# The first batch of an attention-and-maxout kernel: earlier transpositions and products with v, weights prepared at half the rate, four groups in place of six for the first 288 tokens

## The chip, the cores and the metric

The kernel runs on one core of a Trainium2 chip. The time is the device time of one execution in microseconds. The kernel before took 789.06 us in the median of three runs (788.3, 789.06 and 790.6). The profile was taken from one more execution.

A core has five engines with instruction queues of their own: TensorE (PE; its loads of the stationary operand are shown as PEld), VectorE (DVE), ScalarE (ACT), GpSimd (POOL) and SyncE (SP), which here issues most of the transfers (DMA). Every queue is worked in order, and engines wait for one another through semaphores. TensorE writes to PSUM, which is cut into banks.

## The reference

For 8 batches, 8 heads, 576 tokens and a head size of 64:

```python
scores = q @ k.T / 8  - slope[h] * |i - j|        # for 0 <= i - j < 128, else -1e9
attn   = softmax(scores)
x      = (attn @ v), heads side by side           # 4608 tokens x 512
h      = max(x @ w1, x @ w2, x @ w3)              # 512 -> 768
out    = h @ w_out                                # 768 -> 512
```

All of it is in float32. A query sees itself and the 127 tokens before it.

## The kernel before

**Attention.** A task is a batch and a pair of heads, of which a batch has four (`NP`). A task has five blocks of 128 query rows (`NB`, the last has 64). One block of one task is a *step*; a batch has 20. The first batch takes the blocks 0 to 2 of all four tasks first (steps 0 to 11, `FIRST = 3`) and then the blocks 3 and 4 (steps 12 to 19), so that its first 288 tokens are ready before the others. Steps go in pairs. `products` (L334) makes q times k for a pair, into the PSUM tile `scores` or, for every second pair of the first batch, into the banks ps_m0 and ps_m1. `score` masks (DVE, L360 and L363), adds the bias and takes the minimum (DVE, L377) and forms the exponential (ACT, L381) into a tile `p`, of which there are four. `sums_of` (L390, L393) and `normalise` (L400) divide by the sum on DVE; in the first batch block 0 is normalised together with block 1. `turn` transposes the pair on TensorE (L414), copies it out on ACT (L418, L424, L427) and cuts it to the window by two selects on POOL (L430, L434). `mix_first` multiplies with v in the first batch (L448), once for a task's first 384 tokens and once for its last 192, and copies the result to `xk` on ACT (L456). `mix` (L475, L484) does so in the later batches.

**The maxout, first batch.** The 512x768 weights of w1, w2 and w3 are cut into nine groups 0 to 8, w_out into groups 9 to 11. `plain_x(j)` splits the j-th 288 tokens of x into a high and a low part (ACT L501, DVE L502). `plain_unit` (L646) is a unit of six products of 128x128 by 128x288, three for each of two row halves of the weights: high by low, low by high, high by high. A group needs four units for 288 tokens. The units of the groups below `AHEAD` are done for the first 288 tokens, then for the second 288; from `AHEAD` on both halves of the tokens are done group by group. After 72 units come 16 of nine products each with w_out. Every second unit's result goes to DVE (L602, a maximum with the result so far) or ACT (L604).

**The maxout, later batches.** `unit` (L684) uses a scheme of seven products for eight with sums of weights and of inputs; its weights are stored in DRAM while the first two batches run and are streamed back.

**Preparing weights.** `preparing` is one list of steps that is taken up piece by piece. For each of the twelve groups of `A_ORDER` there are two conversion steps (`convert`: ACT L139, DVE L140, ACT L143, DVE L144 and L149, and a store, L150) and two splitting steps (`part`: ACT L153, DVE L154, and stores L177 or L190 to `keep`); then the group two places on is fetched (L133). Afterwards the sums are made. `weights(n, upto)` takes n steps, and more until `upto` are done. Groups 0 to 2, and those from `AHEAD` on, are split whole into a ring of two tiles; groups from 3 below `AHEAD` are split half by half into other tiles, which are free at that time. A splitting step of a group from `AHEAD` on is held back until an earlier group's units are through.

**The order of the work.** Everything is put on a list of events with a time in steps, which is sorted, and a planner takes the instructions in this order, places those that are ready by its own estimate of durations, and so makes the order of each engine's queue. In the first 64 score instructions DVE's order is tied by hand (`follow`), and TensorE's order is tied to the list from event time 50 on (`fix`). `turn` of a pair that begins at step c has the time c + 4.003, the product with v c + 6.001, `plain_x(0)` and the first unit 16.05, `plain_x(1)` 24.05. The units of the first 288 tokens are spread evenly between these two, those behind them up to unit 72 over the time to 46.05. From time 1.2 to 17.2 one step of weights is taken at every step of attention, later one with every odd unit. The functions that the change touches, and what calls them, follow.

## Time and profile before

| | |
|---|---|
| median of three runs | 789.06 us |
| the profiled execution | 785.73 us, of which the span from first to last instruction is 784.0 |
| PE busy | 751.6 us (96%) |
| PEld busy | 670.0 us (85%) |
| DVE busy | 569.5 us (73%) |
| ACT busy | 511.1 us (65%) |
| POOL busy | 171.2 us (22%) |
| transfers | 187.96 MB, 240 GB/s over the span |

A line such as L646 is a line of the kernel. A row of a group or of the timeline names the line, the engine, the operation, the tile that it writes and those that it reads, the shape and the number of instructions; the brackets or the last column say how long the engine was idle before and what it then waited for. The granted clock is the share of TensorE's full clock that the throttle let through.

### The profile page before, as it was taken

To read this page: it belongs to the slowest core of one execution; us is meant where nothing else is said; L and a number is where in the kernel's file an instruction comes from. 1 tells how busy PE (TensorE), PEld (TensorE's weight loads), DVE (VectorE), ACT (ScalarE), POOL (GpSimd) and SP (SyncE) were. 2 spreads that over 40 slices of the span, in tenths; PEclk is the share of its full clock that TensorE was granted. 3 is DMA by queue.
4 is the path that set the end of the run, shared out by engine and by line. 5 is a ranking of instruction groups with operands and counts; after the bars stand their busy time and mean duration, and the time that the engine had idled before them with its cause. 6 is when DMAs were issued, how large, how long until landed. Compare 5 with 4: busy or idle time off the path is not lost.

```text
span 784.0 us, 18084 instructions
## 1 busy us (share of the span) xinstructions
PE 751.6 (96%) x6344; PEld 670.0 (85%) x6344; DVE 569.5 (73%) x1951; ACT 511.1 (65%) x1668; POOL 171.2 (22%) x374
## 2 busy tenths in 40 slices
PE   5779999999999999999999999999999999999997
PEld 2357878888889998899989988999889998999987
DVE  5878989779999477774769567784677657673662
ACT  6867778668778666766677566775677656642331
POOL 1122222111123122212322122221222122201100
PEclk9969999999999999999999999999999999999999
DMA  8887775679897478745887379755887368756851
GB/s 295 292 272 251 231 257 199 200 243 334 303 323 272 140 268 291 263 166 202 284 292 269 118 241 310 251 204 175 293 297 251 135 211 290 243 176 207 290 192 61
DMA packets 54155, 187.96 MB, mean 240 GB/s; under 512 B 5936, under 2 KB 15664, under 8 KB 47152
## 3 DMA queue, kind: packets, MB, share of 16 engines
q0 software_dynamic: 15552, 99.10, 38.4%
q1 hardware_dynamic: 38368, 87.64, 32.5%
q8 instruction: 50, 0.82, 0.4%
q14 instruction: 41, 0.34, 0.1%
q10 hardware_dynamic: 144, 0.07, 0.0%
HBM read 154.53 MB, written 32.24 MB: 238 GB/s over the span
## 4 chain that ended last, share of the span: by engine, by line
PE 60%; DVE 16%; issue 10%; DMA 5%; ACT 5%; POOL 2%; SPq 1%; POOLq 0%; ACTq 0%; DVEq 0%
PE ps_m L684 41%; PE ps_x L475 6%; PE ps_s L334 5%; PE ps_m L646 4%; PE pt L414 4%; DMA hs<-in_w_all 3%; DVE hs L502 2%; DVE t L607 2%; DVE xs L502 2%; ACT p L381 1%; DVE s L377 1%; DVE hq L608 1%; DVE ps_s L363 1%; ACT xs L501 1%; DMA wt<-keep 1%
## 5 line engine op out<-in xcount | busy, mean ns | idle before, releaser
L684 PE MATMUL ps_m<-xs,wt 128*128 128x288 f32 x2646 | 370.4, 297 | 3.9 <-DVE t L607 1.8
L684 PEld LDWEIGHTS ps_m<-xs,wt 128*128 128x128 f32 x2646 | 355.3, 188 | 7.7 <-DVE t L607 3.4
L430 POOL TENSOR_SCALAR_AFFINE_SELECT pp<-pr 128x256 f32<-128x256 f32 (+1 forms) x128 | 56.6, 442 | 385.2 <-ACT pr L427 226.4
L381 ACT ACTIVATE p<-s,st 128x128 f32<-128x128 f32 (+1 forms) x320 | 127.0, 399 | 20.0 <-DVE st L377 18.8
L693 ACT COPY t<-ps_m 128x288 f32<-128x288 f32 x231 | 89.7, 394 | 71.8 <-PE ps_m L684 71.2
L684 PE MATMUL ps_m<-hs,ow 128*128 128x288 f32 x882 | 124.0, 297 | 1.6 <-DVE hs L502 0.8
L684 PEld LDWEIGHTS ps_m<-hs,ow 128*128 128x128 f32 x882 | 118.7, 188 | 3.1 <-ACT t L693 1.1
L285 POOL DMA_DIRECT2D wt<-keep x108 | 58.0, 537 | 193.8 <-PE ps_m L684 189.0
L405 ACT ACTIVATE p<-p,st 128x128 f32<-128x128 f32 (+1 forms) x240 | 84.0, 397 | 17.9 <-DVE st L393 17.8
L377 DVE CUSTOM_DVE_ANT_0 s<-ps_s,bias 128x128 f32<-128x128 f32 (+1 forms) x300 | 76.3, 279 | 19.4 <-PE ps_s L334 17.2
L607 DVE TENSOR_TENSOR t<-ps_m,t 128x288 f32<-128x288 f32 x126 | 56.5, 452 | 36.8 <-PE ps_m L684 20.9
L363 DVE COPY_PREDICATED ps_s<-prev,ps_s 128x256 f32<-128x256 uint8 x120 | 50.6, 421 | 40.6 <-PE ps_s L334 39.2
L334 PE MATMUL ps_s<-qk 64*64 64x192 f32 (+1 forms) x1052 | 64.8, 329 | 6.3 <-DMA qk<-in_qk 4.2
L501 ACT CAST hs<-hq 128x288 fp32r<-128x288 f32 x117 | 48.8, 429 | 29.4 <-DVE hq L608 16.7
L475 PE MATMUL ps_x<-pp,v 128*64 128x256 f32 (+3 forms) x672 | 65.3, 321 | 0.0
L434 POOL TENSOR_SCALAR_AFFINE_SELECT pp<-pr 128x256 f32<-128x256 f32 (+1 forms) x128 | 63.1, 493 | 0.0
L427 ACT COPY pr<-pt 128x256 f32<-128x256 f32 x68 | 20.2, 322 | 64.6 <-PE pt L414 64.6
L381 ACT ACTIVATION_READ_ACCUMULATOR p<-s,st 128x1 f32 (+1 forms) x320 | 61.1, 191 | 0.0
L414 PEld LDWEIGHTS pt<-ident,p 128*128 128x128 f32 (+1 forms) x320 | 34.7, 145 | 28.2 <-issue 17.4
L414 PE MATMUL pt<-ident,p 128*128 128x128 f32 (+1 forms) x320 | 57.4, 292 | 1.3 <-ACT pr L427 0.9
L608 DVE TENSOR_TENSOR hq<-t,hq 128x288 f32<-128x288 f32 x126 | 57.0, 459 | 2.0
L502 DVE TENSOR_TENSOR hs<-hq,hs 128x288 fp32r<-128x288 f32 x117 | 53.1, 460 | 6.2 <-ACT hs L501 6.2
(78 smaller groups left out, 857.7 us busy)
## 6 DMA issues: line engine op xcount, KB each, us to landing
wt<-keep POOLq DMA_DIRECT2D x54, 1024.0 KB, 7.2
wt<-keep POOLq DMA_DIRECT2D x54, 768.0 KB, 5.4
qk<-in_qk SPq DMA_DIRECT2D x29, 576.0 KB, 6.3
hs<-in_w_all SPq DMA_DIRECT2D x24, 512.0 KB, 5.2
v<-in_v SPq DMA_DIRECT2D x30, 320.0 KB, 5.5
outT<-t SPq DMA_DIRECT2D x64, 144.0 KB, 1.8
keep<-wt SPq DMA_DIRECT2D x27, 256.0 KB, 3.8
wt<-keep SPq DMA_DIRECT2D x27, 256.0 KB, 4.4
```

The source lines that it names most:

```text
L334: pe(nc.tensor.matmul(ps[j][d:d + D, o:o + k1 - k0], lhsT=qkt[t][j * D:(j + 1) * D, 0, q0:q0 + D], rhs=qkt[t][j * D:(j + 1) * D, 1, k0:k1] ...
L377: follow(nc.vector.tensor_tensor_reduce(out=s[:n], in0=ps[j][:n, P:2 * P], in1=(bias if i else bias0)[:n, 2 * hp + j, :], scale=-0.125, sc ...
L381: nc.scalar.activation(p[:n, j], s[:n], AF.Exp, bias=st[:n, 0, a, j:j + 1], scale=-1.0, accum_out=st[:n, 1, a, j:j + 1])
L405: nc.scalar.activation(p[:n, j], p[:n, j], AF.Copy, scale=st[:n, 2, a, j:j + 1])
L414: pe(nc.tensor.transpose(out=pt[:, a, j, :n], in_=p[:n, j], identity=ident[:n, :n]))
L434: nc.gpsimd.affine_select(out=w[:n, :, 0, :n], in_=r[:n, a, :, :n], pattern=[[0, 2], [1, n]], compare_op=ALU.is_ge, fill=0.0, base=0, chan ...
L475: pe(nc.tensor.matmul(x[j * D:(j + 1) * D, c:c + e - a], lhsT=vv[:n, i, j * D:(j + 1) * D], rhs=w[:n, j].rearrange("p a b -> p (a b)")[:, ...
L502: e.tensor_tensor(out=lo, in0=src, in1=hi.bitcast(F32), op=ALU.subtract)
L607: nc.vector.tensor_tensor(out=s, in0=ps, in1=e, op=ALU.add)
L608: nc.vector.tensor_tensor(out=h, in0=s, in1=h, op=ALU.max)
L684: pe(nc.tensor.matmul(ps, lhsT=lt, rhs=rt, start=i == 0 and k in (0, 1, 4), stop=i == len(pairs) - 1, skip_group_check=True,))
L693: nc.scalar.copy(out=e, in_=ps)
```

## The change

Three constants of the order are changed, all for the first batch.

- `turn` of the first batch comes at 0.1 behind the last normalisation of its two blocks (`ended`), and no longer 4.003 behind the pair's first step.
- The product with v comes 4.001 and no longer 6.001 behind it (`LAG_X0`); `plain_x(0)`, the first unit (14.05) and `plain_x(1)` (22.05) move by two steps with it. The time at which the second batch's tokens are taken up stays 46.05.
- Weights are prepared at the event times 1.2, 3.2, ... 15.2: eight steps and not seventeen.
- `AHEAD` is 4 and not 6: sixteen units and not twenty-four for the first 288 tokens, then sixteen for the second, then five groups (and not three) for both. Groups 4 and 5 are therefore split whole, into the ring.

```diff
-LAG_T, LAG_X = 4, 6
+LAG_T, LAG_X, LAG_X0 = 4, 6, 4
...
-    AHEAD = 6
+    AHEAD = 4
...
+    def ended(s):
+
+        return max(place_of[t, 1 if i == 0 else i] for t, i in steps[s:s + 2]) + 1.3
+
...
-                at(c + LAG_T + 0.003, turn, place_of[t, i])
+                at(c + LAG_T + 0.003 if b else ended(place_of[t, i]) + 0.1, turn, place_of[t, i])
...
-                    at(c + LAG_X + 0.001, mix_first, t, i == NB - 1)
+                    at(c + LAG_X0 + 0.001, mix_first, t, i == NB - 1)
...
     ready = [n_steps * (b + 1) - 2 + LAG_X + 0.05 + shift[b] for b in range(B)]
-    when = FIRST * NP - 2 + LAG_X + 0.05
+    ready[0] += LAG_X0 - LAG_X
+    when = FIRST * NP - 2 + LAG_X0 + 0.05
     at(when, plain_x, 0)
...
-    for s in range(1, FIRST * NP + LAG_X):
+    for s in range(1, FIRST * NP + LAG_X0, 2):
         at(s + 0.2, weights, 1)
```

## The prediction

> **What bounds the kernel now.** I read the page's busy shares and slices first, then the stretches of the start, then the order of TensorE's work in them, and last the groups of each engine there.

> ```profile
> PE 751.6 (96%) x6344; PEld 670.0 (85%) x6344; DVE 569.5 (73%) x1951; ACT 511.1 (65%) x1668; POOL 171.2 (22%) x374
> PE   5779999999999999999999999999999999999997
> DVE  5878989779999477774769567784677657673662
> ...
> 0.00:53.30 53.30, 34.77 (x222) 17.80 (x223) 39.48 (x162) 38.12 (x121) 12.77 (x30) 0.89 0.84 285
> 10.00:53.30 43.30, 30.58 (x174) 15.35 (x175) 35.71 (x141) 32.72 (x101) 10.47 (x20) 0.87 0.85 294
> 53.30:84.20 30.90, 28.54 (x236) 24.57 (x234) 27.76 (x89) 22.94 (x70) 5.19 (x12) 0.97 0.80 264
> 84.00:110.00 26.00, 25.30 (x227) 22.46 (x228) 24.96 (x96) 20.04 (x65) 6.72 (x12) 1.00 0.73 234
> 84.20:150.00 65.80, 63.46 (x582) 54.80 (x583) 58.81 (x216) 48.47 (x156) 15.51 (x32) 1.00 0.64 208
> 150.00:250.00 100.00, 98.93 (x858) 89.88 (x857) 91.55 (x315) 80.42 (x265) 21.25 (x38) 1.00 0.88 303
> ```

> In a row of stretches stand its length and then the busy time of PE, PEld, DVE, ACT and POOL. TensorE is idle for 32.4 of the 784.0 us, and 18.5 + 2.4 us of that lie before 84.2. Behind 84.2 it is the bound: 2.3 us idle up to 150, 1.1 in the next 100. Ahead of 84.2 the busiest engine is VectorE: 82% of 10 to 53.3, 90% of 53.3 to 84.2, 96% of 84 to 110. So the first batch waits for VectorE (DVE), and everything later for TensorE.

> What TensorE does at the two seams, and DVE's last score of steps 15 and 19:

> ```profile
> 53.34 5.90 PE L646 MATMUL ps_m<-xs,wt 128*128 128x288 f32 x36
> 76.31 0.64 PE L414 MATMUL pt<-ident,p 128*128 128x128 f32 x4
> 81.84 0.97 PE L448 MATMUL ps_x<-pp,hs 128*64 128x128 f32 x10
> 84.25 4.25 PE L646 MATMUL ps_m<-xs,wt 128*128 128x288 f32 x30 [0.73 <-DVE xs L502]
> ...
> 17.43 0.28 DVE L377 CUSTOM_DVE_ANT_0 s<-ps_s,bias 128x128 f32<-128x128 f32 x1
> 49.91 0.28 DVE L377 CUSTOM_DVE_ANT_0 s<-ps_m,bias 64x128 f32<-64x128 f32 x1
> 67.39 0.28 DVE L377 CUSTOM_DVE_ANT_0 s<-ps_m,bias 64x128 f32<-64x128 f32 x1
> ```

> No unit of the maxout starts before 53.3. The 24 units of the first 288 tokens are then through by 81.8, and at 84.25 the second 288 tokens start, having waited for their split on DVE. The last scores of the batch (step 19) were done at 67.7, yet their transposition came at 76.3 and their product with v at 81.8: 14 us of delay behind units. Steps 4 to 15 took from 17.4 to 50.2, so 11 steps at 3.0 us.

> **The change part by part.** I count by DVE's work up to the moment t* at which the second 288 tokens are ready (84.2 now).

> ```profile
> L149 DVE TENSOR_TENSOR hs<-hs 128x512 f32<-128x512 f32 x8 | 5.6, 700 | 1.2 <-ACT hs L143 1.1
> L154 DVE TENSOR_TENSOR wt<-hs,wt 128x512 fp32r<-128x512 f32 x6 | 4.1, 680 | 0.0
> L154 DVE TENSOR_TENSOR ow<-hs,ow 128x256 fp32r<-128x256 f32 x2 | 0.7, 408 | 0.0
> ...
> L149 DVE TENSOR_TENSOR hs<-hs 128x512 f32<-128x512 f32 x7 | 4.9, 699 | 1.9 <-ACT hs L143 1.9
> L140 DVE SCALAR_TENSOR_TENSOR hs<-hs 128x512 int32<-128x512 int32 x7 | 4.7, 677 | 0.0
> L154 DVE TENSOR_TENSOR ow<-hs,ow 128x256 fp32r<-128x256 f32 x10 | 4.4, 463 | 0.4 <-ACT ow L153 0.4
> L602 DVE TENSOR_TENSOR hq<-ps_m,hq 128x288 f32<-128x288 f32 x8 | 3.5, 450 | 0.8 <-PE ps_m L646 0.8
> L144 DVE TENSOR_SCALAR hs<-hs 128x512 int32<-128x512 int32 x7 | 2.9, 413 | 0.0
> L502 DVE TENSOR_TENSOR hs<-hq,hs 128x288 fp32r<-128x288 f32 x3 | 1.3, 442 | 0.0
> L154 DVE TENSOR_TENSOR xs<-hs,xs 128x256 fp32r<-128x256 f32 x2 | 0.8, 413 | 0.0
> L154 DVE TENSOR_TENSOR hs<-hs,hs 128x256 fp32r<-128x256 f32 x2 | 0.7, 406 | 0.0
> ```

> The first three rows are of 0 to 53.3, the others of 53.3 to 84.2. A conversion step costs DVE 0.68 + 0.41 + 0.70 = 1.79 us (L140, L144, L149), a splitting step 0.68, or 0.83 where it is done as two halves of 256. Before 84.2 there were 15 conversions (8 + 7) and 14 splittings (6 whole, and 16 halves): 29 steps.

> *Weights every second step, four groups.* Followed through the code: eight steps are given out ahead of the units in place of 17, and one with every odd unit; at unit 12 two more are forced, since group 3 must be there. At unit 16 that makes 18 steps: 10 conversions and 8 splittings. Until unit 24 nothing more comes, as group 4 takes the ring slot for which unit 23 must be through. So by t* DVE has 5 conversions (9.0 us) and 6 splittings (5.0 us) fewer to do. Eight units fewer mean four results fewer at 0.45 (L602) and two cuts fewer at 0.44: 2.7 us. Together **16.7 us**, and t* would be 84.2 − 16.7 = 67.5, if DVE's idle time (17.0 us before 84.2, 6.2 of it in the first 10) stays. ScalarE loses its share of the same steps and was less busy than DVE in every stretch. Each deferred step takes its two or three transfers on SP's queue along, so the loads of q, k and v that queue behind them go out no later than now.

> *Transpositions and products sooner.* No instruction is added. The transpositions of a pair are issued 0.1 behind its last normalisation and no longer up to 1.6 steps later, the product with v two steps earlier. On TensorE's queue, which is in order, they wait for L400 and the select on POOL with less other work ahead. The benefit is the 14 us tail; a transposition sooner also frees one of the four buffers `p` sooner, for which the score four steps later waits. I price this at nothing beside the 16.7, since DVE, which hides it, is the bound. Without that cover it is worth up to two steps, 6.0 us; the other bound is −3.0 us, one step, where scores of the next pair stand behind a blocked transposition. The earliest units meet one new wait: `products(14)` holds banks ps_m0 and ps_m1 until score 15, so the first unit, though issued at 14.05, can't precede nominal step 15. That keeps half of its gain of two steps, and 3.0 us are not in my sum.

> *What TensorE owes.* Eight units are done after t* and not before.

> ```profile
> 131.60 4.00 PE ps_m L646 x30
> 137.36 3.20 PE ps_m L646 x24
> ...
> L646 PE MATMUL ps_m<-hs,ow x144: 288/294/403, 148.1 to 169.8; 128*128 128x288 f32 x144
> ```

> By the two stretches of the chain a product takes 133 ns, a unit of six 0.80, so 6.4 us are owed. The last row, the products with w_out, has unit 72 at its head: it starts at 148.1. TensorE alone would gain 16.7 − 6.4 = **10.3 us**, and t* = 77.8 is where it gains nothing.

> *What DVE owes.* The 16.7 us come back before unit 72, which starts the w_out products: DVE had 58.8 us of work from 84.2 to 150, now 75.5 from 67.5. At 96%, the share that it reached from 84 to 110, this takes 78.6 us and ends at 146.1: 3.9 us gained. At 100% it is 7.0 gained, at the 89% of the whole stretch 84.5 us and 2.0 lost. I take 96%, the row of the stretch most like it, so **3.9**. Groups 4 and 5 are split whole and not in halves: 4 × 0.15, 0.6 us less on DVE, within this.

> Here is the clock, which the sum leaves alone:

> ```profile
> 40.00:45.00 5.00, 3.75 (x20) 1.81 (x18) 3.89 (x17) 2.72 (x9) 1.93 (x4) 0.50 0.98 352
> ```

> The granted clock was 0.50 while TensorE was 75% busy with attention, and the first 36 products took 164 ns each in place of 133: 1.1 us. [...]

> **The sum.** The profiled execution took 785.73 us, of which 784.0 are span. 784.0 − 3.9 = 780.1, so 781.8 with the 1.7 around it. The three runs' median is 789.06, 3.3 above the profiled one; on that scale the forecast is 789.06 − 3.9 = 785.2, say **785.0**.

> **The rivals.**
> *Full gain.* DVE needn't have all done by unit 72: if what is late is covered by units in hand, only TensorE's account counts, 10.3 us: 778.8. For it: from 150 to 250 TensorE lost 1.1 us with DVE at 92%. Against it: the steps are tied to units, and 48 of them must precede unit 72.

> *Nothing.* If the attention steps run at the latency of their loop (score, exponential, normalisation, transposition, banks) and not at DVE's rate, the freed DVE idles: half of the 16.7 remains, t* = 75.9, TensorE gains 1.9 at most and the owed work of DVE takes it: 788.5. For it:

> ```profile
> DVE st L390 <- ACT p L381: 4.6, 4, 2.0
> ACT xk L456 <- PE ps_x L448: 5.2, 5, 2.0
> ```

> These are waits from 10 to 53.3, DVE for ScalarE's exponential and ScalarE for the product. Against it: 3.0 us a step with DVE at 82% busy.

> *Slower: weights just in time.* Before, 40 steps are out at unit 48 where 32 are needed, and 48 at unit 64 where 44 are. Changed, by the same count: 30 against 32 at unit 48, 36 against 36 at unit 56, 40 against 44 at unit 64; the shortage is issued right ahead of the unit that needs it.

> ```profile
> L139 ACT ACTIVATE hs<-hs 128x512 int32<-128x512 uint32 x7 | 4.8, 681 | 0.6 <-DMA hs<-in_w_all 0.6
> L143 ACT ACTIVATE hs<-hs 128x512 int32<-128x512 f32 x7 | 4.8, 685 | 0.1
> L153 ACT CAST wt<-hs 128x512 fp32r<-128x512 f32 x6 | 3.7, 615 | 0.0
> ACT hs L139 <- DMA hs<-in_w_all: 4.9, 4, 2.6
> ```

> Two splittings cost 0.62 + 0.68 + 0.68 = 2.0 us; at unit 64 a whole group comes, 0.68 + 0.68 + 0.69 + 0.41 + 0.70 for the first conversion, 1.79 for the second and 2.0 to split: 6.9. Units 12, 48 and 64 make 10.9 us, and behind TensorE's stopped unit stand the transpositions and scores of batch 1, so DVE starves too. Uncovered, 10.9 − 3.9 = 7.0 lost, 796; half covered, 1.6 lost, 790.6; I set this case at 793. It decides once the stops at these units pass 3.9 us. For it: ScalarE already waited 4.9 us for raw weights from 84.2 to 150 (last row), with the larger lead. Against it: ScalarE and DVE may run ahead of TensorE, whose units take 0.8 us each.

> **How the numbers follow.** Forecast 0.44, full gain 0.18, nothing 0.20, slower 0.18. A difference under 0.3% (2.4 us) can't be told from none. The forecast's spread (shares of 100% to 95%, 782 to 786) and the full gain lie over that: 0.62 faster; the third case is the 0.20 of no change; the slower case gives 0.18. From 778 (full gain) to 792 (the slower case nearly half covered) the range leaves out its uncovered part and a gain beyond 11.

> **What would show it.** Right: first L646 near 44 (53.3 less 4 conversions and 3 splittings, 9.4 us) and at the latest 50; the 97th product of L646 near 67 and with it L502 of the second tokens; DVE over 95% busy from there to 146. Last score to last product with v under 8 us shows the sooner issue. Wrong: DVE idle over 8 us between 10 and the first unit (nothing gained); PE idle before L646 behind L154 at units 12, 48 or 64 (slower); L646's last unit of the first batch (its last product now starts at 169.8) less than 2 us earlier would refute the sum whatever the cause.

## The result and the profile after

The changed kernel takes 796.69 us (median of four executions, 793.49 to 799.23) against 788.68 for the kernel before (788.0 to 790.6). The ratio is 1.0091, with a 95% interval of 1.0063 to 1.0119: **slower by 0.9%**, about 8 us. I had forecast 785.0, faster, and the time lies above the top of my range (792). The profiled execution of the changed kernel is the longest of its four: 799.23 us, span 797.5. Ratios, here and below, are of executions in the fast state; two in the slow one (801.4 us of e2, 900.9 us of e11) count in the medians only.

Engine shares and slices of the changed kernel's page:

```profile
PE 761.9 (96%) x6344; PEld 675.8 (85%) x6344; DVE 568.7 (71%) x1947; ACT 510.7 (64%) x1664; POOL 176.3 (22%) x374
...
PE   5897999899999999999999999999999999999887
...
DVE  5876899689999566784778567784778567674562
```

The work is the same to a few instructions, and TensorE is busy 10 us longer. TensorE's slices differ from those before up to 80 us and in the eighth (140 to 160 us). Here are the two stretches of the first batch, first of the kernel before, then of the changed kernel (columns: length; busy time of PE, PEld, DVE, ACT, POOL; granted clock; share of the transfer engines; GB/s):

```profile
30.00:80.00 50.00, 40.60 (x295) 29.46 (x288) 42.52 (x155) 37.27 (x118) 11.49 (x24) 0.86 0.79 264
80.00:150.00 70.00, 66.98 (x625) 57.53 (x624) 63.01 (x229) 52.09 (x165) 15.51 (x32) 1.00 0.64 210
```

```profile
30.00:80.00 50.00, 43.48 (x287) 31.23 (x287) 36.70 (x141) 32.48 (x103) 14.74 (x24) 0.83 0.55 185
80.00:150.00 70.00, 63.86 (x549) 53.23 (x548) 60.35 (x210) 49.00 (x148) 16.62 (x28) 0.96 0.74 252
```

VectorE, which I took for the bound from 10 to 110 us, is *less* busy than before (36.7 of 50 us, was 42.5), and TensorE does its work at a lower clock in both stretches. So neither engine is full. The order of TensorE in the changed kernel, with the last row from its list of groups:

```profile
36.86 0.91 PE L646 MATMUL ps_m<-xs,wt 128*128 128x288 f32 x5
51.15 0.75 PE L448 MATMUL ps_x<-pp,v 128*64 128x192 f32 x6 [1.17 <-POOL pp L430]
71.75 0.44 PE L448 MATMUL ps_x<-pp,hs 128*64 128x128 f32 x4 [2.17 <-POOL pp L430]
72.87 1.32 PE L448 MATMUL ps_x<-pp,hs 128*64 128x192 f32 x8 [0.68 <-POOL pp L430]
74.11 1.81 PE L646 MATMUL ps_m<-xs,wt 128*128 128x288 f32 x6
76.10 4.82 PE L646 MATMUL ps_m<-xs,wt 128*128 128x288 f32 x24 [0.18 <-DVE xs L502]
...
L646 PE MATMUL ps_m<-hs,ow x144: 288/294/403, 156.7 to 178.4; 128*128 128x288 f32 x144
```

The first unit starts at 36.86 (was 53.34), earlier than the 44 that I named. But the second 288 tokens are there only at 76.1 (the unit at 74.1 is the first on them), not at 67.5. At 76.10, 102 of the products of L646 are done, at 84.25 before it was 144; the 42 missing ones are 42 × 0.133 = 5.6 us, so of 8.15 us at the seam 2.5 are a gain. From there to the start of the last product with w_out the changed kernel needs 178.4 − 76.1 = 102.3 us, where the kernel before with those 5.6 us added would need 85.55 + 5.6 = 91.15: 11.2 us lost. Together the first batch ends 8.6 us later, close to the difference of the medians (8.0). The profiled spans differ by 13.5; the other 4.9 lie in later batches. That remainder of the span is 614.2 us before and 619.1 after, and 614 to 619 in all the profiles below; I don't explain it.

The forecast counted VectorE's work up to the start of the second 288 tokens and let its idle time there stay at 17.0 us. From the start to the first unit on these tokens, before and changed (VectorE's busy time is the third pair):

```profile
0.00:84.25 84.25, 63.31 (x456) 42.38 (x456) 67.30 (x251) 61.11 (x190) 17.96 (x42) 0.92 0.82 278
0.00:74.11 74.11, 57.26 (x392) 35.75 (x392) 52.28 (x211) 47.68 (x154) 20.87 (x42) 0.92 0.70 240
```

Its work shrank by 15.0 us, near the 16.7 that I counted. Its idle time did not stay: it rose from 17.0 to 21.8 us.

### The profile page after: what moved, and what is told of

Its sections match the earlier page's. It is cut to its first block, busy times and chain, and to the rows that moved or that the text cites. A ratio compares the mean times of both kernels' runs of the same rounds, so it can differ in the third digit from the quotient of the medians.

```text
span 797.5 us, 18069 instructions
## 1 busy us (share of the span) xinstructions
PE 761.9 (96%) x6344; PEld 675.8 (85%) x6344; DVE 568.7 (71%) x1947; ACT 510.7 (64%) x1664; POOL 176.3 (22%) x374
## 4 chain that ended last, share of the span: by engine, by line
PE 59%; DVE 14%; issue 9%; ACT 4%; POOL 2%; DMA 2%; SPq 0%; POOLq 0%; DVEq 0%; ACTq 0%
PE ps_m L684 43%; PE ps_x L475 5%; PE ps_s L334 4%; PE pt L414 3%; PE ps_m L646 3%; DVE hs L502 2%; DVE t L607 2%; DVE xs L502 2%; ACT p L381 1%; DVE hq L608 1%; POOL pp L434 1%; DVE s L377 1%; DMA wt<-keep 1%; DVE ps_s L363 1%; ACT xs L501 1%
## 5 line engine op out<-in xcount | busy, mean ns | idle before, releaser
L684 PE MATMUL ps_m<-xs,wt 128*128 128x288 f32 x2646 | 372.0, 298 | 7.1 <-DMA wt<-keep 3.4
L684 PEld LDWEIGHTS ps_m<-xs,wt 128*128 128x128 f32 x2646 | 356.7, 189 | 11.2 <-DVE t L607 3.0
L430 POOL TENSOR_SCALAR_AFFINE_SELECT pp<-pr 128x256 f32<-128x256 f32 (+1 forms) x128 | 59.9, 468 | 388.8 <-ACT pr L427 228.5
L381 ACT ACTIVATE p<-s,st 128x128 f32<-128x128 f32 (+1 forms) x320 | 127.1, 400 | 19.8 <-DVE st L377 18.7
L377 DVE CUSTOM_DVE_ANT_0 s<-ps_s,bias 128x128 f32<-128x128 f32 (+1 forms) x300 | 76.1, 279 | 19.1 <-PE ps_s L334 17.5
L475 PE MATMUL ps_x<-pp,v 128*64 128x256 f32 (+3 forms) x672 | 67.1, 322 | 5.1 <-POOL pp L430 5.0
L334 PE MATMUL ps_s<-qk 64*64 64x192 f32 (+1 forms) x1052 | 66.8, 333 | 4.7 <-DMA qk<-in_qk 4.2
L434 POOL TENSOR_SCALAR_AFFINE_SELECT pp<-pr 128x256 f32<-128x256 f32 (+1 forms) x128 | 65.0, 508 | 0.0
L646 PE MATMUL ps_m<-xs,wt 128*128 128x288 f32 x384 | 63.5, 322 | 0.7 <-DVE wt L154 0.5
L646 PEld LDWEIGHTS ps_m<-xs,wt 128*128 128x128 f32 x384 | 57.8, 208 | 4.1 <-issue 2.5
L381 ACT ACTIVATION_READ_ACCUMULATOR p<-s,st 128x1 f32 (+1 forms) x320 | 61.2, 191 | 0.0
L475 PEld LDWEIGHTS ps_x<-pp,v 128*64 128x64 f32 (+1 forms) x672 | 38.7, 135 | 25.6 <-issue 9.0
```

Source lines behind the costliest of these rows:

```text
L334: pe(nc.tensor.matmul(ps[j][d:d + D, o:o + k1 - k0], lhsT=qkt[t][j * D:(j + 1) * D, 0, q0:q0 + D], rhs=qkt[t][j * D:(j + 1) * D, 1, k0:k1] ...
L377: follow(nc.vector.tensor_tensor_reduce(out=s[:n], in0=ps[j][:n, P:2 * P], in1=(bias if i else bias0)[:n, 2 * hp + j, :], scale=-0.125, sc ...
L381: nc.scalar.activation(p[:n, j], s[:n], AF.Exp, bias=st[:n, 0, a, j:j + 1], scale=-1.0, accum_out=st[:n, 1, a, j:j + 1])
L430: nc.gpsimd.affine_select(out=pp[t, i - 1][:, :, 1, :n], in_=r[:, a, :, :n], pattern=[[0, 2], [-1, n]], compare_op=ALU.is_gt, fill=0.0, ba ...
L434: nc.gpsimd.affine_select(out=w[:n, :, 0, :n], in_=r[:n, a, :, :n], pattern=[[0, 2], [1, n]], compare_op=ALU.is_ge, fill=0.0, base=0, chan ...
L475: pe(nc.tensor.matmul(x[j * D:(j + 1) * D, c:c + e - a], lhsT=vv[:n, i, j * D:(j + 1) * D], rhs=w[:n, j].rearrange("p a b -> p (a b)")[:, ...
```

## The experiments

Four questions were put: which of the three parts costs the time; whether it is the weights that come just in time (my slower rival) or the sooner order; what stops the engines; and what a select on POOL costs beside VectorE. The results for the first question stand in one table. "Lost clock" is (1 − mean granted clock) × span, in the median over the executions of a kernel: the time by which TensorE ran short of its full clock.

| groups first / preparation / lags | run | median us, of before | ratio [95%] | seam | last w_out | lost clock |
|---|---|---|---|---|---|---|
| 6, every step, old | before | 789.2 | 1 | 84.25 | 169.8 | 9.4 |
| 6, every step, sooner | e4 | 787.17, 789.32 | 0.9989 [0.9962, 1.0017] | 81.22 | 168.9 | 7.1 |
| 6, every second, old | e7 | 788.54, 789.22 | 0.9995 [0.9971, 1.0018] | 78.81 | 169.2 | 6.3 |
| 6, every second, sooner | e1 | 786.98, 789.32 | 0.9970 [0.9945, 0.9996] | 78.56 | 166.9 | 4.7 |
| 4, every step, old | e3 | 793.47, 789.32 | 1.0048 [1.0021, 1.0076] | 77.39 | 173.9 | 11.1 |
| 4, every step, sooner | e5 | 793.43, 789.27 | 1.0052 [1.0029, 1.0075] | 75.36 | 170.3 | 9.5 |
| 4, every second, old | e6 | **783.44**, 789.27 | **0.9928 [0.9902, 0.9954]** | 66.34 | 163.7 | 1.6 |
| 4, every second, sooner | changed | 796.69, 788.68 | 1.0091 [1.0063, 1.0119] | 74.11 | 178.4 | 14.7 |

"Seam" is the start of the first unit on the second 288 tokens, "last w_out" that of the last product with w_out in the first batch, both in the one profiled execution. The list of preparation times ends with `LAG_X0`. So "every step" is seventeen steps ahead of the units with the old lags and fifteen with the sooner ones, and "every second" is nine and eight.

### One part undone or done alone

**e1**, six groups, the rest of the change kept:

```diff
-    AHEAD = 4
+    AHEAD = 6
```

> The changed kernel with AHEAD back at 6: transpositions and products sooner, weights every second step, six groups. Theory A (the loss is the burst: with four groups four weight steps are forced at unit 64, their run on VectorE holds up POOL's select, TensorE stands 3.7 us at the product with v and then runs at half clock): by the count of steps nothing is forced behind unit 20, so no select of POOL over 2 us between 100 and 160 us, and the time is 788 or less. Rival B (the sooner issue or the thinner preparation does it, whatever the groups): 795 to 798, as changed.

Measured: 0.9970, three tenths of a per cent faster. With six groups the other two parts are harmless.

**e2**, one step of weights with each of the units 24 to 39 and not with every second, so that none has to be forced at units 48 and 64:

```diff
-        weights(v % 2, 4 * (A_ORDER.index(g) + 1) if g < 9 else 48)
+        weights(1 if 24 <= v < 40 else v % 2, 4 * (A_ORDER.index(g) + 1) if g < 9 else 48)
```

> The changed kernel, with one weight step at every unit from 24 to 39 and not at every second: eight steps earlier, so that by the count nothing is forced at units 48 and 64; everything else as changed. Theory A: the long select near 139 us and the 3.7 us stop go, the w_out products start 5 to 9 us earlier than 156.7, the time is 787 to 791. Rival B: no effect, 795 to 798. Rival C (VectorE has simply too much to do between 76 and 150 us): the same work earlier only moves the stops, 794 to 797.

Measured: 792.4 us, 1.0025 [0.9992, 1.0058]. That is 4.3 us less than the changed kernel, but not the time before: forced weights are a part of the loss at most.

**e3**, four groups alone, on the kernel before:

```diff
-    AHEAD = 6
+    AHEAD = 4
```

> The kernel before with only AHEAD = 4. By the count of steps two are forced at unit 48 and four at unit 64, just as in the changed kernel. Theory A: a run of VectorE with a select over 2 us ahead of the w_out products and a stop of TensorE of some 3 us with the half clock behind it; without the sooner start 792 to 798. Rival B: within 1 us of before, 789.

Measured: 1.0048, slower. Its seam is 6.9 us earlier than before, about the 6.4 us that the eight units moved take, so nothing is gained there, as I read it because the weights are still prepared ahead of it.

**e4**, the sooner order alone (the changed kernel with six groups and a step of weights at every step of attention):

```diff
-    AHEAD = 4
+    AHEAD = 6
...
-    for s in range(1, FIRST * NP + LAG_X0, 2):
+    for s in range(1, FIRST * NP + LAG_X0):
```

> The kernel before with only the sooner transpositions and products (six groups, a weight step at every step of attention). Theory A: no forced steps, so nothing lost, and the earlier start of the units gives 1 to 3 us: 785.5 to 788.5. Rival B, if the sooner issue does the harm: 793 to 797.

Measured: 0.9989, no difference that can be told.

**e5**, the changed kernel without the half rate (only the second edit of e4):

> The changed kernel with a weight step at every step of attention again (four groups and sooner issue kept). By the count two steps are forced at unit 48 and four at unit 64, none at unit 12. Theory A (four groups cause the loss by the forced steps at the end): 1.003 to 1.008 of before, as with four groups alone. Rival (the halved rate is what makes four groups worse): within 0.3% of before.

Measured: 1.0052, the same as e3. At full rate the sooner order makes no difference with four groups either.

**e6**, the changed kernel with the old lags:

```diff
-LAG_T, LAG_X, LAG_X0 = 4, 6, 4
+LAG_T, LAG_X, LAG_X0 = 4, 6, 6
...
-                at(c + LAG_T + 0.003 if b else ended(place_of[t, i]) + 0.1, turn, place_of[t, i])
+                at(c + LAG_T + 0.003, turn, place_of[t, i])
```

> The changed kernel with the old lags of transposition, product and first unit (four groups and the halved rate kept). By the count the same steps are forced as in the changed kernel, at units 12, 48 and 64. Theory A: 1.005 to 1.012 of before. If the sooner issue is what makes four groups worse, 1.003 or less.

Measured: 783.44 us, 0.9928 [0.9902, 0.9954], **the fastest kernel here, ahead of both**. Beside the changed kernel it differs in when transpositions, products with v and the first units are issued, and in one step of weights more ahead of the units (nine and not eight). Together that is worth 1.0091 − 0.9928 = 1.6%, 13 us.

**e7**, the half rate alone (e6 with `AHEAD = 6`):

> The kernel before with only the halved preparation (nine steps ahead of the units in place of 17; six groups, old lags). If the sooner issue is what does harm wherever preparation is halved, this is faster than with the sooner issue added (0.997): 0.988 to 0.994. If it harms only together with four groups: 0.996 to 1.000.

Measured: 0.9995, nothing. Its seam is 5.4 us earlier than before, but the last product with w_out only 0.6: what is deferred is given back. So no part alone gains, and none alone loses more than 0.5%. Four groups and the half rate gain 0.7% together; the sooner order gains a little or nothing in three of the four places of the table and costs 1.6% in the fourth.

What e6 does up to its seam, in the two stretches, in TensorE's order, and the start of its w_out products:

```profile
0.00:66.34 66.34, 50.28 (x408) 32.11 (x408) 52.68 (x215) 49.82 (x165) 19.53 (x42) 1.00 0.76 258
30.00:80.00 50.00, 43.70 (x389) 34.81 (x389) 45.40 (x175) 38.52 (x125) 14.73 (x28) 1.00 0.65 212
80.00:150.00 70.00, 65.20 (x562) 55.10 (x561) 62.90 (x214) 53.39 (x157) 16.47 (x29) 1.00 0.80 273
...
42.41 3.44 PE L646 MATMUL ps_m<-xs,wt 128*128 128x288 f32 x24
...
L646 PE MATMUL ps_m<-hs,ow x144: 288/294/402, 140.9 to 163.7; 128*128 128x288 f32 x144
```

VectorE does 45.4 us in 50 (the changed kernel 36.7), TensorE finishes 389 matmuls in the same busy time in which the changed kernel finishes 287, and the clock is full in both stretches.

### Which half of the sooner order

**e8**, only the transposition sooner (the first edit of e6 alone):

> Four groups and the halved rate, with the transpositions sooner but the old lags of the product with v and of the first unit. Theory B1 (the earlier units hold the banks ps_m0 and ps_m1 that the scores of step 18 need): 0.990 to 0.995, as with the old lags, and the second 288 tokens are split by 66 to 68 us. Theory B2 (waits without slack in the in-order queues of TensorE and ScalarE, behind transposition and product): partly worse, 0.996 to 1.004.

Measured: 784.59 us, 0.9946 [0.9927, 0.9964], with 2.3 us of lost clock: as e6.

**e9**, transposition and product with v sooner, the first units and the split of the tokens at their old times:

```diff
-    ready[0] += LAG_X0 - LAG_X
-    when = FIRST * NP - 2 + LAG_X0 + 0.05
+    when = FIRST * NP - 2 + LAG_X + 0.05
```

> The changed kernel, but the splits of x and the first units keep their old times (16.05 and 24.05); transpositions and products with v stay sooner. Theory B1: the harm is gone, 0.990 to 0.996, the products of q and k of step 18 (L334 into ps_m) are not scattered over 5 us and more between units. Theory B2: the harm stays, 1.003 to 1.010, with ScalarE's copy L456 waiting over 6 us for the product with v up to 76 us, as in the changed kernel (7.7; 2.1 with the old lags).

Measured: 790.25 us, 1.0004 [0.9988, 1.0021], lost clock 4.7. That lies between the ranges of the two theories, so neither accounts for all of the loss.

**e10**, product with v and units one step sooner and not two, transposition at its old time:

```diff
-LAG_T, LAG_X, LAG_X0 = 4, 6, 4
+LAG_T, LAG_X, LAG_X0 = 4, 6, 5
...
-                at(c + LAG_T + 0.003 if b else ended(place_of[t, i]) + 0.1, turn, place_of[t, i])
+                at(c + LAG_T + 0.003, turn, place_of[t, i])
```

> Four groups and the halved rate, old transpositions, product with v and units one step sooner and not two. Both theories: between the old lags (0.9928) and the changed kernel (1.009); if the loss comes from units ahead of step 18's scores, near the old lags, 0.990 to 0.996, since the first unit then stands behind score 15 anyway; if from the product's wait, near 1.001.

Measured: 789.07 us, 1.0008 [0.9981, 1.0036], lost clock 5.5. So the transposition is free, the product with v two steps sooner costs some 6 us (784.59 to 790.25), and the units with it another 6 (to 796.69).

One thing goes along with the first 6 us: e6 and e8 take nine steps of weights ahead of the units, e9, e10 and the changed kernel eight. No run holds this number while it moves the product. The stops shown next make it unlikely as the cause: they lie at 48 to 56 us, ahead of unit 12 (62.27), the first that one step less can hold up by my count. Between e9 and the changed kernel the number is the same.

The waits of 30 to 80 us, of the changed kernel, of e9, of e6 and of the kernel before (engine, tile, line, whom it waited for: us in total, times, longest):

```profile
ACT xk L456 <- PE ps_x L448: 7.7, 4, 3.6
PE ps_x L448 <- POOL pp L430: 5.8, 6, 2.2
DVE st L390 <- ACT p L381: 4.7, 4, 2.2
```

```profile
ACT xk L456 <- PE ps_x L448: 7.2, 6, 3.6
PE ps_x L448 <- POOL pp L430: 4.8, 7, 1.8
DVE st L390 <- ACT p L381: 4.1, 5, 1.5
```

```profile
PE ps_x L448 <- POOL pp L430: 2.9, 3, 1.7
ACT xk L456 <- PE ps_x L448: 2.1, 2, 1.2
DVE st L390 <- ACT p L381: 1.5, 2, 1.1
```

```profile
PE ps_x L448 <- POOL pp L430: 6.1, 7, 1.6
ACT xk L456 <- PE ps_x L448: 4.1, 4, 2.0
DVE st L390 <- ACT p L381: 3.6, 3, 2.0
```

Among the kernels with four groups and the half rate, the waits at L448 go with the time: 2.9 us in e6 and 1.8 in e8 (783 and 785 us), 4.2 in e10 and 4.8 in e9 (789 and 790), 5.8 in the changed kernel. The kernel before has as much of them, 6.1 us, with the old lags: they are not new, but the two parts that help take half of them away (e6), and the sooner product brings them back.

Three queues stop one another. One such place of the changed kernel, engine by engine:

```profile
48.38 1.10 POOL L430 TENSOR_SCALAR_AFFINE_SELECT pp<-pr 128x256 f32<-128x256 f32 x1 [4.50 <-ACT pr L427]
...
52.00 0.32 ACT L456 COPY xk<-ps_x 128x192 f32<-128x192 f32 x1 [3.52 <-PE ps_x L448]
...
53.13 0.16 DVE L390 TENSOR_SCALAR st<-st 64x2 f32<-64x2 f32 x1 [2.19 <-ACT p L381]
...
56.16 0.49 DVE L360 COPY_PREDICATED ps_m<-prev,ps_m 128x128 f32<-128x128 uint8 x2 [2.19 <-PE ps_m L334]
```

The selects run from 48.38 to 51.33. The product with v at the head of TensorE's queue waits for them (the 1.17 us at 51.15 above); behind it stand the products q times k of step 18, so its score comes at 56.16 (in e6 at 49.16; in e2, where the clock stayed full, at 54.34). ScalarE's copy of the product has been at the head of *its* queue since 48.5, and behind it stand the exponentials for which VectorE waits. VectorE then stands 2 × 2.19 = 4.4 us within 6; of the second 2.19, e2 has only 0.33, so most of it is the clock (below). In e6 VectorE has no gap over 0.1 us from 45.6 to 54.5. I call such a chain of stops a convoy.

The longest of the waits at L448, 2.17 us at 71.75, just ahead of the seam, has another cause beside the order. The select that it waits for lasted 2.57 us, from 69.12 on, while VectorE converted weights without a gap up to 71.42. In e2, which does the same instructions up to there, that select took 0.72 us and the wait was 0.31: the order makes such a stop possible, and timing decides whether it comes.

### The clock

The column of lost clock points at a second price. In the ten executions of e1, nine of e2 and ten of e10 the time rises by 0.97, 0.87 and 1.10 us with each us of lost clock (correlations 0.85, 0.83, 0.90); in the others by 0.3 to 1.6 (e4), and in the kernel before by 0.1 to 0.5 with correlations under 0.4. The instructions of e2 and of the changed kernel are the same in the same order on every engine until unit 24, behind the seam, and the two profiled executions agree within 0.06 us from 36 to 51.9 (earlier within 0.52). Then the clock is halved in one and not in the other; the changed kernel first, then e2:

```profile
48.50:51.91 3.41, 2.12 (x21) 0.90 (x19) 2.44 (x10) 0.00 (x0) 2.83 (x4) 1.00 0.93 272
51.91:55.32 3.41, 3.41 (x18) 2.22 (x13) 0.84 (x3) 3.32 (x9) 0.00 (x0) 0.50 0.97 383
...
54.37 1.75 PE L334 MATMUL ps_m<-xs 64*64 64x256 f32 x6
...
58.03 1.09 PE L334 MATMUL ps_s<-qk 64*64 64x128 f32 x14
```

```profile
47.33:50.74 3.41, 2.57 (x17) 1.48 (x15) 3.41 (x13) 1.20 (x6) 2.31 (x3) 1.00 0.94 281
50.74:54.15 3.41, 2.96 (x25) 1.80 (x25) 1.07 (x4) 2.11 (x7) 0.64 (x2) 1.00 0.99 386
...
53.33 0.97 PE L334 MATMUL ps_m<-xs 64*64 64x256 f32 x6
...
55.35 0.77 PE L334 MATMUL ps_s<-qk 64*64 64x128 f32 x14
```

The same instructions start 2.7 us later by 58.0. No edit lies between the two here: behind the same convoy the clock is 0.50 in one execution and 1.00 in the other. (Why the rows have these borders is told in the last section.)

So of the 13 us between e6 and the changed kernel, two prices add up: the convoys (e9 against e6: 6.8 us, with 3.1 us of lost clock), and what the sooner units add (the changed kernel against e9: 6.4 us, with 10.0 us more lost clock). That the clock costs time is shown for the 2.7 us above; for the rest of the second price it goes with the time and was not changed by itself. A rival stands beside it: in the changed kernel the products q times k of step 18 lie scattered between units, from 48.77 to 56.1 us, in e9 together, from 51.53 to 53.7, as theory B1 of the earlier units had it. No run parts the two.

### Weights just in time

The longest stop of TensorE in the changed kernel's first batch comes behind 66 units, next to unit 64, where four steps of weights are forced, as the slower rival counted:

```profile
139.10 4.15 POOL L434 TENSOR_SCALAR_AFFINE_SELECT pp<-pr 128x256 f32<-128x256 f32 x1
139.17 0.67 DVE L149 TENSOR_TENSOR hs<-hs 128x512 f32<-128x512 f32 x1
...
142.25 0.74 DVE L502 TENSOR_TENSOR xs<-xk,xs 128x576 fp32r<-128x576 f32 x1
...
143.67 0.76 PE L475 MATMUL ps_x<-pp,v 128*64 128x256 f32 x2 [3.70 <-POOL pp L430]
146.81 2.77 PE L646 MATMUL ps_m<-xs,wt 128*128 128x288 f32 x10
...
145.00:150.00 5.00, 5.00 (x28) 3.50 (x28) 1.58 (x4) 0.43 (x1) 0.00 (x0) 0.50 0.01 3
```

TensorE stands for 3.70 us, but not for the weights. It waits for a select on POOL that lasts 4.15 us (the median select takes 0.40), as long as seven VectorE instructions, six of weight steps and a split (L502), run without a gap, from 139.17 to 142.99. Behind the stop the clock is 0.50 from 144.07 to 150.90 us, which is 3.4 us of lost clock, and ten products take 277 ns each and not 133.

**e11** tells whether the forced steps alone do harm: e2's line on e6.

> Four groups, halved rate, old lags, and one weight step at every unit from 24 to 39, so that by the count nothing is forced at units 48 and 64. If the forced run of VectorE at unit 64 costs what its long selects suggest (2.1 and 3.6 us long, TensorE waiting 1.7 us): 0.989 to 0.992 of before. If the run is covered by other work of TensorE: 0.992 to 0.996.

Measured: 784.03 us, 0.9941 [0.9919, 0.9964], against e6's 0.9928: nothing gained by taking the forced steps away. In e6 the same thing happens (POOL and PE of e6):

```profile
128.21 3.56 POOL L434 TENSOR_SCALAR_AFFINE_SELECT pp<-pr 128x256 f32<-128x256 f32 x1
...
128.31 0.65 PE L475 MATMUL ps_x<-pp,v 128*64 128x256 f32 x2 [0.57 <-POOL pp L430]
132.18 0.65 PE L475 MATMUL ps_x<-pp,v 128*64 128x256 f32 x4 [1.11 <-POOL pp L430]
```

A select of 3.56 us, but TensorE has other work ahead of that product, waits 1.7 us in two pieces, and keeps its clock (1.00 from 80 to 150 us). Whether the 4.3 us that e2 gains come from this stop stays open: its profile shows 2.10 us of wait there in place of 3.70, but it was already 3.8 us ahead at the seam, before its edit.

### A select beside VectorE

Four kernels put extra work on VectorE beside the selects of batches 3 and 4, on the kernel before, behind the copy of the transposed block. **p1** adds 14 maxima of 128 elements with two operands in SBUF, **p2** the same with one of them in PSUM:

```diff
+            if 3 * NP <= steps[s][0] < 5 * NP:
+                for _ in range(14):
+                    nc.vector.tensor_tensor(out=dist, in0=r[:, 0, 0], in1=r[:, 0, 1], op=ALU.max)
```

(in p2 `in0=pt[:, 0, 0]`)

> The kernel before, with 14 more additions of work on VectorE behind each copy of a whole transposed pair in batches 3 and 4: maxima of two 128x128 operands, both in SBUF, into a tile that is no longer used. The output is the reference's. If a run of VectorE instructions with two SBUF operands holds up GpSimd's select, some selects L430 or L434 in these batches (about 340 to 520 us) last 2 to 4 us, where the kernel before has a median of 0.40.

> The same 14 maxima in the same places, but one operand is the transposed pair in PSUM. If it is the second SBUF operand that holds up the select, the selects in these batches stay near 0.40 us though VectorE is as busy; if any busy VectorE does it, they last 2 to 4 us as with two SBUF operands.

Measured, one execution each: 789.46 and 789.22 us beside 789.27; the selects of 128x256 of the second line take, from 300 to 420 us, 509 and 502 ns in the mean where the kernel before shows 484. The two hardly differ, and no select there is over 1.2 us: with instructions this small the question stays open. **p3** adds eight of the weights' own kind (L140's, 512 elements, two operands in SBUF), **p4** twelve with one operand and constants (L144's kind):

```diff
+            if 3 * NP <= steps[s][0] < 5 * NP:
+                b32 = bias.rearrange("p h k -> p (h k)").bitcast(I32)
+                for _ in range(8):
+                    nc.vector.scalar_tensor_tensor(
+                        out=b32, in0=b32, scalar=0, in1=b32, op0=ALU.logical_shift_left, op1=ALU.bitwise_or,
+                    )
```

(in p4 `range(12)` and `tensor_scalar(out=b32, in0=b32, scalar1=-1, scalar2=0, op0=ALU.bitwise_and, op1=ALU.bitwise_xor)`)

> The kernel before, with eight more operations of VectorE at each transposition of a whole pair in batches 3 and 4: the instruction of line 140 (two operands in SBUF, 512 elements), written so that it leaves its tile as it was. The output is the reference's. If long instructions with two SBUF operands, one behind the other, hold up the select: some selects of 2 us or more between 300 and 420 us. If only the other kind does: none over 1.2 us (the longest there before is 0.97).

> The same with twelve operations of the kind of line 144 (one operand in SBUF and immediates, 512 elements in 0.42 us). If this kind holds up the select: some selects of 2 us or more between 300 and 420 us. Otherwise none over 1.2 us.

Measured: 795.70 and 795.52 us, one execution each, beside 789.15. The selects from 300 to 420 us (count, then total us and mean ns) of the kernel before, of p3 (L440 is L434 there), with one place of its timeline, and of p4:

```profile
L434 POOL TENSOR_SCALAR_AFFINE_SELECT pp<-pr 128x256 f32<-128x256 f32 x15 | 7.3, 484 | 0.0
```

```profile
L440 POOL TENSOR_SCALAR_AFFINE_SELECT pp<-pr 128x256 f32<-128x256 f32 x16 | 13.1, 817 | 0.0
...
347.28 2.25 POOL L440 TENSOR_SCALAR_AFFINE_SELECT pp<-pr 128x256 f32<-128x256 f32 x1
347.31 0.68 DVE L422 SCALAR_TENSOR_TENSOR bias<-bias 128x512 int32<-128x512 int32 x1
348.58 1.49 DVE L422 SCALAR_TENSOR_TENSOR bias<-bias 128x512 int32<-128x512 int32 x2
```

```profile
L440 POOL TENSOR_SCALAR_AFFINE_SELECT pp<-pr 128x256 f32<-128x256 f32 x16 | 8.2, 515 | 0.0
```

On this line the long two-operand instructions add 0.33 us to the mean select and hold one for 2.25 us; about as much one-operand work (12 × 0.41 = 4.9 us beside 8 × 0.68 = 5.4) adds 0.03. On the first line (L430, 424 ns before) p3 has 486 and p4 528. Over both lines the mean rises from 457 ns to 653 in p3 and 519 in p4, and only p3 has a select over 1.2 us in this stretch. So VectorE's load alone does little, and long instructions of L140's kind do more. That it is their second SBUF operand is not shown: the two kinds are also different operations, each was run once, and the kernel before has one select of 2.32 us too (at 244 us). The two times are equal within what a single execution tells, so no price of a late select follows from them.

## Why the prediction was wrong

**The bound.** That VectorE's work sets the seam held where the queues let VectorE run: in e6 it is busy 91% of 30 to 80 us. It did not hold for the changed kernel, where it is busy 73%: up to the seam it stood idle 21.8 us, where the prediction's condition was that its idle time stays at 17.0. "DVE, which hides it, is the bound" was an argument from the kernel before, in which the sooner product doesn't exist yet.

**Weights every second step, four groups.** This step was right in direction and near in size, shown by e6, which does only this (with nine steps ahead and not eight): t* was put at 67.5 and is 66.34. That it lies so near is partly luck: VectorE's work fell by 14.6 us (67.30 to 52.68) and not by 16.7, and its idle time by 3.3 (17.0 to 13.7), which I had held fixed. 6.4 us owed at the seam leave 17.9 − 6.4 = 11.5 us (forecast 10.3); of these 5.4 are given back up to w_out (97.4 us in place of 85.55 + 6.4), where I had 6.4. Net 6.1 us in the profile and 5.8 between medians, for 3.9 forecast. The whole profiled spans differ by 2.3 us only (784.0 and 781.7), as the profiled execution of the kernel before is 3.5 us faster than its median of 789.27. Part of the gain goes with the clock: the kernel before loses 0.14 × 50 = 7.0 us in 30 to 80, e6 none, and my sum "leaves alone" the clock.

**Transpositions and products sooner** is the step that failed: "I price this at nothing beside the 16.7", with bounds of −3.0 and +6.0 us. It costs 13 us beside the other two parts (one step of weights goes along with it). The text named the wait (the product, in TensorE's in-order queue, behind the select on POOL) and then took "less other work ahead" for a benefit. It is the cause of the loss: with less work ahead, the product reaches the head before its input is there, and the queue behind it stops. I had not named the other in-order queue, ScalarE's, whose copy of the product stands ahead of exponentials. The lower bound, one step, was for a single blockade; the profile has six waits at L448 (5.8 us), four at L456 (7.7 us), and the clock on top. That they follow one another through the queues is read from the place at 48 to 56 us; for the other stops it is inferred.

In the terms of the sum: t* came at 74.11 and not at 67.5, 6.6 us late: nearly all of it is VectorE's added idle time, 4.8, and work that I overcounted, 1.7. Behind it 6.4 us were to be given back up to w_out; it was 178.4 − 74.1 − 85.55 − 6.4 = 12.4, 6.0 more. TensorE's lost clock there is as large (5.1 us at half clock from 74.11 and 6.8 from 144.07, so 6.0), where the kernel before has none. So the forecast gain of 3.9 us became a loss of 8.6.

**The first unit** came at 36.86 and not at 44 or later: I had put step 15 as its limit, for the banks that step 14's products hold; but it starts before step 14's last score (38.93), and only the units behind it come at 41.08. It bought nothing: the 16 units of the first 288 tokens are through by 69.6, as the products of step 18 and the stopped products with v stand between them, and TensorE then waits for the last product with v and the split of the second 288 tokens.

**The clock** was left out of the sum, which so took it to stay as it was (1.1 us on the first 36 products). Lost clock rose from 9.4 to 14.7 us in the medians. In the profile it is 11.9 us up to the last product with w_out: the clock was 0.50 from 51.91 to 58.73, 62.15 to 65.56, 72.39 to 79.22 and 144.07 to 150.90 us, so 1.7 or 3.4 us each time. Before, it was 6.8 us, all ahead of the seam.

**The rivals.** "Full gain" and "nothing" did not come. "Weights just in time" had the right sign and one right place (unit 64), and its 793 lay nearer than the forecast, but its mechanism is not the main one: TensorE waits there for a select, its waits for L154, the sign that I set, come to 0.5 us in the first batch, and e11 shows that the forced steps cost nothing under the old lags. "Last score to last product with v under 8 us" would have shown the sooner issue right; it is 14 us still (step 19's score at 59.0, the product at 72.9), and the refutation that I set, L646's last product less than 2 us earlier, came in plainly: 8.6 us later.

## What to carry to other kernels

An instruction issued sooner on an in-order queue is only free if its inputs are sure to be there when it reaches the head (from 30 to 80 us the product with v waited 5.8 us at the head of TensorE's queue, and its copy 7.7 us at the head of ScalarE's): look for the slowest producer (here a select on POOL), for what stands behind the consumer on its own queue and behind its reader on the next, and leave the lag where inputs arrive late. Parts that are harmless alone can cost 1.6% together, so try a change of several parts with each part undone; here undoing one of three turned 0.9% slower into 0.7% faster. Compute (1 − granted clock) × span for every execution: where the time rises with it by about 1 us per us, as in e1, e2 and e10, the clock goes along with the spread between executions; in the kernel before it hardly does.

## What the runs showed of the hardware

**Some selects on POOL lasted as long as a run of VectorE instructions.** 2.25, 2.57, 3.56 and 4.15 us were seen above for a select of 0.40. The kind of instruction goes with it on the second line, each in one execution: 817 ns in the mean with long two-operand instructions, 515 with one-operand ones. At 139.10 the select ended, at 143.25, only when seven VectorE instructions in a row had ended (142.99), two of them (L144) with a single operand. The select of p3 that began at 347.28 ended at 349.53, just behind the first gap of VectorE, of 0.04 us at 349.26. So in these two places the select lasted through the whole run without a gap; what in the run held it is not shown. Most selects are not held so long: ten of p3's took 0.84 to 0.86 us.
